# The order of the first loads and of the first matmuls in an S5 and SwiGLU kernel

## The chip, the cores and the metric

The kernel runs on one core of a Trainium2 chip. The metric is the device time of one execution in microseconds. Before the change it is 177.39 us, the median of 3 runs (177.05 to 178.04).

Engine names: TensorE (PE in the profile; PEld is its weight load), VectorE (DVE), ScalarE (ACT), GpSimd (POOL) and SyncE (SP), whose queue issues most transfers.

## What is computed

The input x has 2048 tokens of 512 features, in bf16. Two branches work on its layer norm, and both are added to x:

```python
def _A_ref(x, Lambda_re, Lambda_im, B_re, B_im, C_re, C_im, log_dt, Dskip):
    Lam = Lambda_re + 1j * Lambda_im
    dt = jnp.exp(log_dt)
    Lam_bar = jnp.exp(dt * Lam)
    B_bar = ((Lam_bar - 1.0) / Lam)[:, None] * (B_re + 1j * B_im)
    Bu = jnp.einsum("bld,pd->blp", x + 0j, B_bar)
    hs, h = [], jnp.zeros_like(Bu[:, 0, :])
    for t in range(L):
        h = Lam_bar[None, :] * h + Bu[:, t, :]
        hs.append(h)
    hseq = jnp.stack(hs, 1)
    return 2.0 * jnp.einsum("blp,dp->bld", hseq, C_re + 1j * C_im).real + x * Dskip

def _B_ref(x, w_gate, w_up, w_down):
    return (silu(x @ w_gate) * (x @ w_up)) @ w_down

xn = _layernorm(x)
return x + _A_ref(xn, ...) + _B_ref(xn, ...)
```

The state has 512 entries; gate and up have 1376 features, which is ten blocks of 128 and a last one of 96.

## The kernel before

The tokens are 16 tiles of 128 (`NT`), four to a chunk (`NCH` is 4, `TPC` is 4). The features of x are four blocks of 128 (`KD`; `HK` is half of it, 2). Chunk by chunk the kernel computes the projection with B (`bproj_tile`, eight of four matmuls per chunk), the rotations and scans on VectorE (`ssm_ops`), gate and up (`gateup_tile`, `gateup_last` for the last 96 features), and at the end the product with w_down and C (`out_ffn`, `out_ssm`). Every engine runs its instructions in the order in which the program issues them. VectorE's work of the scans and tables lies in a list with costs (`queue`), and each block of matmuls takes as much from it as it pays for (`pump`); products of gate and up wait in the list `products` until `multiply` issues them.

Chunk 0 is treated differently, and the change touches it alone. While its weights are still on their way, TensorE would have nothing to do; so gate and up of its tiles are computed with the tokens as the stationary operand and 512 features of a weight row as the moving one (`sw_mm`). A weight row here is one block of 128 input features with the first 1024 output features, 256 KB (`load_row`); up has rows 0 to 3 in `wu01`, gate in `wg01`. The rest, output features 1024 to 1375 of both, is `w_end`.

Tiles 0 and 1 do not wait for their layer norm. TensorE transposes the raw tile by a matmul with the identity (`raw_mm`, L237) and subtracts the mean by a second matmul into the same bank (`cT_mean`, L245), whose stationary operand is a row sum that VectorE made (`sum_dve`, L229). ScalarE and VectorE copy the four blocks of the result to `xcT` (`raw_copy`, L252); the scale 1/std is applied when the results leave their banks (`sw_up`, L526; `sw_gate`, L514). `cT_mean(i, k, k + 2)` does two blocks with one matmul. The eight banks of `pair` hold up and gate of two tiles and two groups of 512 features; the transposes borrow banks of it before they are used.

The order of loads on SyncE's queue: tile 0 (L128), the four up rows, gate rows 0 and 1, tile 2, gate row 2, tile 3, gate row 3, `w_end`, chunk 1 of x. Tile 1 is issued on ScalarE's queue (L130), behind a memset of two elements on VectorE. The parameters of the state are three small loads on GpSimd's queue (L145).

The order of TensorE: nine dummy matmuls (L703), transposes of tile 0, its first two means, transposes of tile 1, the other means, then the four up rows, each for tile 0 and tile 1 and both feature groups (`row_mm(0, k)`, four matmuls, L506), then the gate rows. Between them lie the transposes of tile 2, which is centred on VectorE (`center`, L226). After the layer norms of tiles 0 to 3 (`ln_stats` L189, `ln_rstd` L198 and L199, `norm_dve` L207) two transposing transfers on SyncE make `xnT0`, tile 3 first (L258), and behind them the same queue loads and transposes B (`load_bt`, L150). Tiles 2 and 3 and `w_end` follow on TensorE (L506, L805), then chunk 0's projection (L387), then `gateup_last(0)` (L555), which reads `xnT0` and `w_end` in 16 matmuls of 192 columns, then chunk 1's projection. The part of the program from the projection on:

```python
    need("ln0")
    for part in range(2):
        for q in range(NQ):
            bproj_tile(0, part, q)
...
    need("ln1")
    g0_dma(0, fgroups[1][1])
    gateup_last(0)
    pump(GU / 2)
    bproj_chunk(1)
```

Of the kernel before, what the change touches and what calls it, by code (L numbers as in the profile page):

```python
# [23 lines left out]
def kernel(  # L24
# [17 lines left out]
    nc = tc.nc  # L42
# [9 lines left out]
    KD = D // 128  # L52
# [25 lines left out]
    def bank(shape=(128, CW), dtype=F32):  # L78
        return psum.tile(list(shape), dtype, name="ps")

    def flat(ap3):
        return ap3.rearrange("p q j -> p (q j)")

    x_v = A_x[0].rearrange("(n p) d -> p n d", p=128)
    out_v = out[0].rearrange("(n p) d -> p n d", p=128)
    wg_v = B_w_gate.rearrange("(k p) f -> p k f", p=128)
    wu_v = B_w_up.rearrange("(k p) f -> p k f", p=128)


    xall = const.tile([128, NT, D], BF16, name="xall")  # L90
# [5 lines left out]
    wu01 = const.tile([128, KD, FE], BF16, name="wu01")  # L96
# [24 lines left out]
    def load_row(q, t, view, k):  # L121
        q.dma_start(out=t[:, k, :], in_=view[:, k, 0:FE])  # L122

    HK = KD // 2
# [1 line left out]
    make_identity(nc, ident[:])  # L126
    minus_mean = const.tile([128, 128], BF16, name="minus_mean")
    nc.sync.dma_start(out=xall[:, 0, :], in_=x_v[:, 0, :])  # L128
    nc.vector.memset(xall[:, 1, 0:2], 0.0)
    nc.scalar.dma_start(out=xall[:, 1, :], in_=x_v[:, 1, :])  # L130
    nc.scalar.preload_act_table_set("silu_and_others")
    for k in range(KD):
        load_row(nc.sync, wu01, wu_v, k)
    for k in range(HK):
        load_row(nc.sync, wg01, wg_v, k)
# [49 lines left out]
    def by_k(ap):  # L185
        return ap.rearrange("p (k d) -> p k d", d=128)
# [36 lines left out]
    sums = const.tile([128, 2], BF16, name="sums")  # L223
# [4 lines left out]
    def sum_dve(i, dst):  # L228
        nc.vector.scalar_tensor_tensor(out=xnT[:, NCH - 1, i, 0:HW], in0=xall[:, i, 0:HW], scalar=1.0,  # L229
                                       in1=xall[:, i, HW:D], op0=ALU.mult, op1=ALU.add, accum_out=dst)  # L230
# [3 lines left out]
    raw = [pair[0][1] + pair[1][0], pair[1][1] * 2]  # L234

    def cT_mm(ps, src, k, first, stop):
        nc.tensor.matmul(ps[:, k * 128:(k + 1) * 128], lhsT=src[:, k * 128:(k + 1) * 128], rhs=ident[:], start=first,  # L237
                         stop=stop)

    def raw_mm(i):  # L240
        for k in range(KD):
            cT_mm(raw[i][k], xall[:, i, :], k, all(p is not raw[i][k] for p in raw[i][:k]), False)

    def cT_mean(i, *ks):
        nc.tensor.matmul(by_k(raw[i][ks[0]][:])[:, ks[0]:ks[-1] + 1:HK], lhsT=sums[:, i:i + 1].to_broadcast([128, 128]),  # L245
                         rhs=minus_mean[:, None, :].to_broadcast([128, len(ks), 128]), start=False, stop=True)

    def raw_copy(i, k):
        cT_copy(V.tensor_copy if k % 2 else nc.scalar.copy, raw[i][k], i, k, k + 1)

    def cT_copy(copy, ps, i, k0=0, k1=KD):
        copy(out=xcT[:, k0:k1, i * 128:(i + 1) * 128], in_=by_k(ps[:, k0 * 128:k1 * 128]))  # L252
# [21 lines left out]
    V = nc.vector  # L274
# [107 lines left out]
    def bproj_tile(c, part, q):  # L382
        if c not in u_tiles:
            u_tiles[c] = ssm.tile([128, 2, NQ, CW], BF16, name="u16", bufs=2)
        ps = bank()
        for k in range(KD):
            nc.tensor.matmul(ps[:] if c else by_k(ps[:]), lhsT=BT[:, part, k, q * 128:(q + 1) * 128],  # L387
                             rhs=xnT[:, c, k, :] if c else xnT0[:, k], start=(k == 0), stop=(k == KD - 1))
        nc.scalar.copy(out=u_tiles[c][:, part, q, :], in_=ps[:])  # L389
# [67 lines left out]
    products = []  # L457
# [10 lines left out]
    def gu_tile(c):  # L468
        if c not in gu_tiles:
            gu_tiles[c] = gut.tile([128, FT, CW], BF16, name="guT")  # L470
        return gu_tiles[c]
# [8 lines left out]
    def gu_rest(c):  # L480
        return gu_more_rest[:] if c == 2 else gu_tile(c)[:, FT - 1, 0:RT * 128]
# [21 lines left out]
    def sw_mm(ps, groups, gi, i, k0=0, k1=KD):  # L503
        a, b = fgroups[gi]
        for k in range(k0, k1):
            nc.tensor.matmul(ps[:, 0:(b - a) * 128], lhsT=tokens(i, k), rhs=groups[gi][:, k, 0:(b - a) * 128],  # L506
                             start=(k == 0), stop=(k == KD - 1))
# [35 lines left out]
    def g0_dma(a, b):  # L543
        nc.sync.dma_start_transpose(out=runs(gu_tiles[0][:, a:b, :]), in_=g0[:, a:b].rearrange("p f i d -> p (f i d)"))
# [3 lines left out]
    def gateup_last(c):  # L548
        gl = g_last[c % 2][:] if c else g0[:, FT - 1, 0:RT]
        u = up_p.tile([128, RT, 128], BF16, name="ul", bufs=2)  # L550
        for h in range(0, TPC, 2):
            ps = bank()[:, 0:4 * FR].rearrange("p (i w f) -> p i w f", i=2, w=2)
            for i in range(2):
                for k in range(KD):
                    nc.tensor.matmul(ps[:, i],  # L555
                                     lhsT=xnT[:, c, k, (h + i) * 128:(h + i + 1) * 128] if c else xnT0[:, k, h + i, :],
                                     rhs=w_end[:, k, :, FL - FE:FL - FE + FR], start=(k == 0), stop=(k == KD - 1))
            two = slice(h * RB, (h + 2) * RB)
            src = ps.rearrange("p i w (j f) -> p w j i f", f=RB)
            nc.scalar.activation(out=gl[:, :, two].rearrange("p j (i f) -> p j i f", f=RB), in_=src[:, 0], func=ACT.Silu)  # L560
            nc.scalar.copy(out=u[:, :, two].rearrange("p j (i f) -> p j i f", f=RB), in_=src[:, 1])

        def product():
            V.tensor_tensor(out=gl, in0=gl, in1=u[:], op=ALU.mult)
            if c:
                nc.sync.dma_start_transpose(out=gu_rest(c).rearrange("p (n t) -> p n t", t=128),
                                            in_=gl.rearrange("p i d -> p (i d)"))
            else:
                a = fgroups[1][1]
                n = (FT - 1 - a) * TPC + RT  # L570
                nc.sync.dma_start_transpose(
                    out=flat(gu_tile(0)[:, a:FT, :])[:, 0:n * 128].rearrange("p (n t) -> p n t", t=128),
                    in_=g0[:, a:FT].rearrange("p f i d -> p (f i d)")[:, 0:n * 128])
        products.append(product)
# [93 lines left out]
    def step():  # L668
        for item in backlog[0:AHEAD + 1]:
            if item[2] is not None:  # L670
                item[2]()
                item[2] = None
        cost, op, _, _ = backlog.pop(0)
        op()
        owed[0] -= cost

    def pump(us):

        owed[0] += us
        while backlog and owed[0] >= backlog[0][0] * 0.5:  # L680
            step()
        if not backlog:
            owed[0] = 0.0

    def multiply(keep):

        while len(products) > keep:
            products.pop(0)()
            owed[0] -= 0.65

    def need(tag):

        while any(item[3] == tag for item in backlog):
            step()


    GU = 8 * 0.2163
# [29 lines left out]
    dummy(warm, 4, CW)  # L727
    dummy(warm, 5, 128)
    nc.vector.tensor_scalar(out=minus_mean[:], in0=ident[:], scalar1=-1.0 / D, scalar2=None, op0=ALU.mult)
    for i in range(2):  # L730
        sum_dve(i, sums[:, i:i + 1])
    raw_mm(0)
    for k in range(HK):
        cT_mean(0, k)
        raw_copy(0, k)
    raw_mm(1)
    for k in range(HK, KD):
        cT_mean(0, k)
    for k in range(HK):
        cT_mean(1, k, k + HK)  # L740
        raw_copy(1, k)
    for k in range(HK, KD):
        raw_copy(0, k)
    for k in range(HK, KD):
        raw_copy(1, k)

    def row_mm(which, k):
        for i in range(2):
            for gi in range(2):
                sw_mm(pair[which][i][gi], (U, G)[which], gi, i, k, k + 1)  # L750

    for k in range(KD):
        row_mm(0, k)
    for i in range(2):
        ln_stats(i)
        ln_rstd(i, i + 1)
# [3 lines left out]
    for n in range(2):  # L760
        norm_dve(n)
    row_mm(1, 0)
    pp = prm_transpose()
    ln_stats(2)
# [6 lines left out]
    for k in range(1, SW):  # L771
        row_mm(1, k)
# [48 lines left out]
    def bproj_chunk(c):  # L821
        need(f"ln{c}")
        for part in range(2):
            for q in range(NQ):
                bproj_tile(c, part, q)
                pump(BP)
                multiply(0 if q else 1)
# [34 lines left out]
        queue(f"ssm{c}", fwd + back)  # L862

    need("ln0")
    for part in range(2):
        for q in range(NQ):
            bproj_tile(0, part, q)
            pump(BP)
            multiply(0 if q else 1)
# [5 lines left out]
    queue("cf", c_ops())  # L875
    need("ln1")
    g0_dma(0, fgroups[1][1])
    gateup_last(0)
    pump(GU / 2)
    bproj_chunk(1)  # L880
    load_down()
    for part, src in enumerate((A_C_re, A_C_im)):
# [62 lines left out]
```

## Time and profile before

| | us |
|---|---|
| median of 3 runs | 177.39 |
| lowest and highest | 177.05, 178.04 |
| the profiled execution, its own time | 178.12 |
| its span, first to last instruction | 176.0 |
| TensorE busy | 171.0 |
| VectorE busy | 157.4 |
| ScalarE busy | 102.3 |
| all matmuls of chunk 0's last 96 features | 1.32 |

The profile is of one execution. A row of the timeline gives the start and the length in microseconds, the engine, the line of the kernel, the operation, what is written and read, how many instructions were merged into the row, and in brackets how long the engine stood idle before it and what ended that. A row of the chain gives start, length and what the end of the program hung on in that time. A row of transfers ends with the median time from issue to landing. A row of a table of stages gives the stage, its length, the busy time of PE, PEld, DVE, ACT and POOL with the number of instructions, the granted share of TensorE's clock, the busy share of the transfer engines and the GB/s that they moved. [...]

### The profile page before, as it was taken

What the parts mean: (1) busy time and instruction counts of PE and PEld (TensorE: products, weight loads), DVE (VectorE), ACT (ScalarE), POOL (GpSimd) and SP (SyncE); (2) the same over time, 40 slices, a digit from 0 to 9 for tenths busy, and PEclk for the clock granted to TensorE, in tenths of its full rate; (3) what the DMA queues carried; (4) which work ended last, traced back from release to release, by engine and by line L of the source; (5) the groups of instructions that cost most, each with busy time, mean ns of one, the idle gap of its engine ahead of it and who ended that gap; (6) DMA issues with size and microseconds to landing.
All of it is one profiled execution on the core that took longest, in us unless ns stands there. A gap on an engine that the chain in (4) does not pass through costs nothing.

```text
span 176.0 us, 2435 instructions
## 1 busy us (share of the span) xinstructions
PE 171.0 (97%) x878; PEld 82.0 (47%) x894; DVE 157.4 (89%) x260; ACT 102.3 (58%) x188; POOL 27.1 (15%) x36
## 2 busy tenths in 40 slices
PE   8899999999999999999999999999999999999993
PEld 5444445564444464444444444446444444444542
DVE  3767999999999999999999999999999999589642
ACT  3179589794996689976044362014666652983100
POOL 5234110022000000000302500014100000530700
PEclk9999999999999999999999999999999999999999
DMA  5998969999999300220005830006310000597741
GB/s 152 370 342 80 194 110 181 303 202 293 169 207 274 115 4 0 50 61 0 2 4 111 94 34 0 0 4 68 53 22 0 0 4 0 70 164 124 93 89 60
DMA packets 34027, 18.05 MB, mean 103 GB/s; under 512 B 24512, under 2 KB 32832, under 8 KB 33888
## 3 DMA queue, kind: packets, MB, share of 16 engines
q1 hardware_dynamic: 30272, 14.39, 35.0%
q0 software_dynamic: 3456, 3.28, 14.6%
q10 hardware_dynamic: 288, 0.23, 0.4%
q8 instruction: 7, 0.11, 0.3%
q14 instruction: 4, 0.03, 0.1%
HBM read 8.33 MB, written 5.24 MB: 77 GB/s over the span
## 4 chain that ended last, share of the span: by engine, by line
PE 94%; DMA 3%; issue 1%; SPq 0%; ACT 0%; DVE 0%; ACTq 0%
PE ps L462 29%; PE ps L630 20%; PE ps L643 16%; PE ps L387 16%; PE ps L506 7%; PE ps L555 3%; DMA wu<-in_B_w_up_dram 3%; PE ps L805 2%; PE ps L620 2%; ACT u L489 0%; SPq L122 0%; SPq L128 0%; DVE xall L646 0%; PE ps L237 0%; PE ps L278 0%
## 5 line engine op out<-in xcount | busy, mean ns | idle before, releaser
L429 DVE TENSOR_TENSOR_SCAN g<-r_t,car,u 128x512 bf16<-128x512 f32 x24 | 28.8, 1263 | 0.0
L643 PE MATMUL ps<-CF,wt 128*128 128x512 bf16 (+2 forms) x133 | 28.2, 366 | 0.2
L387 PE MATMUL ps<-xnT,BT 128*128 128x512 bf16 x125 | 28.1, 379 | 0.2
L630 PE MATMUL ps<-wd_sb,guT 128*128 128x512 bf16 (+2 forms) x129 | 26.5, 362 | 0.1
L462 PE MATMUL ps<-xnT,wu 128*128 128x512 bf16 x94 | 24.5, 379 | 0.2
L462 PE MATMUL ps<-xnT,wg 128*128 128x512 bf16 x93 | 24.3, 379 | 0.1
L389 ACT CAST u<-ps 128x512 bf16<-128x512 f32 x32 | 17.8, 591 | 5.0 <-PE ps L387 4.1
L489 ACT CAST u<-ps 128x512 bf16<-128x512 f32 x30 | 17.8, 592 | 4.8 <-PE ps L462 4.8
L643 PEld LDWEIGHTS <-wt 128*128 128x128 bf16 x136 | 12.9, 98 | 15.0 <-DVE xall L600 0.4
L387 PEld LDWEIGHTS <-BT 128*128 128x128 bf16 x128 | 12.5, 98 | 14.9 <-DMA BT<-in_A_B_re_dram 0.3
L630 PEld LDWEIGHTS <-guT 128*128 128x128 bf16 x130 | 12.4, 98 | 13.8
L199 POOL TENSOR_TENSOR rstd<-ve,neg_half 128x1 f32<-128x1 f32 (+1 forms) x7 | 7.0, 1001 | 73.0 <-DVE ve L198 72.6
L652 ACT CAST res<-ps 128x512 bf16<-128x512 f32 x12 | 6.9, 582 | 18.5 <-PE ps L643 18.5
L592 ACT ACTIVATE xr<-xall,nb,rstd 128x512 bf16<-128x512 bf16 x16 | 11.8, 804 | 8.7 <-DVE xall L600 5.0
L653 POOL DMA_DIRECT2D out_dram<-res x12 | 10.5, 1043 | 35.6 <-ACT res L652 30.0
L462 PEld LDWEIGHTS <-wu 128*128 128x128 bf16 x96 | 9.4, 98 | 11.3
L488 ACT ACTIVATE guT<-ps 128x512 bf16<-128x512 f32 x20 | 12.1, 604 | 4.0 <-PE ps L462 3.6
L462 PEld LDWEIGHTS <-wg 128*128 128x128 bf16 x96 | 9.3, 98 | 10.6
L212 ACT ACTIVATE xn<-xall,nb,rstd 128x512 bf16<-128x512 bf16 x8 | 6.3, 816 | 8.8 <-DVE nb L202 8.8
L189 DVE BATCH_NORM_STATS2 stats<-xall 128x6 f32<-128x512 bf16 x16 | 10.8, 675 | 0.6 <-DMA xall<-in_A_x_dram 0.6
L462 PE MATMUL ps<-xnT,w_end 128*128 128x512 bf16 x47 | 10.8, 379 | 0.1
L397 DVE TENSOR_TENSOR pm<-g,c 128x2048 bf16<-128x2048 bf16 x8 | 9.8, 1222 | 0.1
(132 smaller groups left out, 235.3 us busy)
## 6 DMA issues: line engine op xcount, KB each, us to landing
out_dram<-in_A_x_dram SPq DMA_DIRECT2D x8, 192.0 KB, 3.2
out_dram<-res POOLq DMA_DIRECT2D x12, 128.0 KB, 3.1
out_dram<-xall POOLq DMA_DIRECT2D x3, 512.0 KB, 6.4
wd_sb<-in_B_w_down_dram SPq DMA_DIRECT2D x1, 1280.0 KB, 7.8
wu<-in_B_w_up_dram SPq DMA_DIRECT2D x4, 256.0 KB, 4.9
wg<-in_B_w_gate_dram SPq DMA_DIRECT2D x4, 256.0 KB, 5.5
xall<-in_A_x_dram SPq DMA_DIRECT2D x1, 1024.0 KB, 7.0
xall<-in_A_x_dram SPq DMA_DIRECT2D x1, 512.0 KB, 6.1
```

The source lines that it names most:

```text
L189: nc.vector.bn_stats(out=stats[:, n, 0, :], in_=xall[:, n, :])
L387: nc.tensor.matmul(ps[:] if c else by_k(ps[:]), lhsT=BT[:, part, k, q * 128:(q + 1) * 128], rhs=xnT[:, c, k, :] if c else xnT0[:, k], star ...
L389: nc.scalar.copy(out=u_tiles[c][:, part, q, :], in_=ps[:])
L429: V.tensor_tensor_scan(out=g()[:, part, q, :], data0=r_t[:, q:q + 1].to_broadcast([128, CW]), data1=u_tiles[c][:, part, q, :], initial=ini ...
L462: nc.tensor.matmul(ps[:fs, lo:hi], lhsT=wslice(groups, fi, k), rhs=xnT[:, c, k, lo:hi], start=(k == 0), stop=(k == KD - 1))
L488: nc.scalar.activation(out=gu(c, fi, fi + 1)[:fs, 0, :], in_=psg[:fs], func=ACT.Silu)
L489: nc.scalar.copy(out=u_pair[c][:fs, fi % 2, :], in_=psu[:fs])
L506: nc.tensor.matmul(ps[:, 0:(b - a) * 128], lhsT=tokens(i, k), rhs=groups[gi][:, k, 0:(b - a) * 128], start=(k == 0), stop=(k == KD - 1))
L592: nc.scalar.activation(out=box["xr"][:], in_=xall[:, n, :], func=ACT.Identity, scale=rstd[:, n:n + 1], bias=nb[:, n:n + 1])
L630: nc.tensor.matmul(o_tiles[n, b][:, 0:hi - lo], lhsT=gu(c, fi, fi + 1)[:, 0, i * 128:(i + 1) * 128], rhs=wd_sb[:, fi, lo:hi], start=(fi == ...
L643: nc.tensor.matmul(o[:, 0:hi - lo], lhsT=w_tiles[c][:, part, q, i * 128:(i + 1) * 128], rhs=CF[:, part, q, lo:hi], start=False, stop=(part ...
L653: nc.gpsimd.dma_start(out=out_v[:, n, lo:hi], in_=res[:, lo:hi], accum_op=ALU.add)
```

## The change

Four things are changed.

1. Tile 1's load moves from ScalarE's queue to SyncE's, behind up rows 0 and 1 and in front of up rows 2 and 3. The memset before it goes.
2. TensorE transposes tile 0 and subtracts all four means, then does up rows 0 and 1 for tile 0 alone. Then come tile 1's transposes and means, row 2 for tile 0, rows 0 to 2 for tile 1, and row 3 for both.
3. VectorE forms tile 1's row sum behind its two copies of tile 0. Its copies of tile 1 go to ScalarE, which now does six of eight.
4. `gateup_last(0)` moves in front of chunk 0's projection. Its product and the transfer behind it keep their place in the order of VectorE and SyncE: the entry is taken out of `products` and put back later.

```diff
     nc.sync.dma_start(out=xall[:, 0, :], in_=x_v[:, 0, :])
-    nc.vector.memset(xall[:, 1, 0:2], 0.0)
-    nc.scalar.dma_start(out=xall[:, 1, :], in_=x_v[:, 1, :])
     nc.scalar.preload_act_table_set("silu_and_others")
-    for k in range(KD):
+    for k in range(HK):
+        load_row(nc.sync, wu01, wu_v, k)
+    nc.sync.dma_start(out=xall[:, 1, :], in_=x_v[:, 1, :])
+    for k in range(HK, KD):
         load_row(nc.sync, wu01, wu_v, k)
...
     def raw_copy(i, k):
-        cT_copy(V.tensor_copy if k % 2 else nc.scalar.copy, raw[i][k], i, k, k + 1)
+        cT_copy(V.tensor_copy if k % 2 and i == 0 else nc.scalar.copy, raw[i][k], i, k, k + 1)
...
-    for i in range(2):
-        sum_dve(i, sums[:, i:i + 1])
+    def row_mm(which, k, tiles=range(2)):
+        for i in tiles:
+            for gi in range(2):
+                sw_mm(pair[which][i][gi], (U, G)[which], gi, i, k, k + 1)
+
+    sum_dve(0, sums[:, 0:1])
     raw_mm(0)
-    for k in range(HK):
+    for k in range(KD):
         cT_mean(0, k)
         raw_copy(0, k)
+    for k in range(HK):
+        row_mm(0, k, (0,))
+    sum_dve(1, sums[:, 1:2])
     raw_mm(1)
-    for k in range(HK, KD):
-        cT_mean(0, k)
     for k in range(HK):
         cT_mean(1, k, k + HK)
+    for k in range(KD):
         raw_copy(1, k)
-    for k in range(HK, KD):
-        raw_copy(0, k)
-    for k in range(HK, KD):
-        raw_copy(1, k)
-
-    def row_mm(which, k):
-        for i in range(2):
-            for gi in range(2):
-                sw_mm(pair[which][i][gi], (U, G)[which], gi, i, k, k + 1)
-
-    for k in range(KD):
-        row_mm(0, k)
+    row_mm(0, HK, (0,))
+    for k in range(HK + 1):
+        row_mm(0, k, (1,))
+    row_mm(0, KD - 1)
...
     need("ln0")
+    gateup_last(0)
+    pump(GU / 2)
+    last0 = products.pop()
     for part in range(2):
...
     g0_dma(0, fgroups[1][1])
-    gateup_last(0)
-    pump(GU / 2)
+    products.append(last0)
     bproj_chunk(1)
```

## The prediction

> **What bounds the kernel now.** I began with the page's busy times, went on to the chain that ended last in order of time, then to the waits of TensorE, and last to a table of stages cut where the chain changes its kind.
>
> ```profile
> span 176.0 us, 2435 instructions
> PE 171.0 (97%) x878; PEld 82.0 (47%) x894; DVE 157.4 (89%) x260; ACT 102.3 (58%) x188; POOL 27.1 (15%) x36
> 1.65 4.80 DMA wu<-in_B_w_up_dram
> 6.49 3.61 PE ps L506 x16
> 23.33 6.91 PE ps L387 x32
> 30.24 1.32 PE ps L555 x16
> PE ps L506 <- DMA wu<-in_B_w_up_dram: 0.6, 1, 0.6
> 4.82:6.49 1.67, 1.07 (x5) 0.43 (x4) 1.39 (x5) 0.60 (x3) 0.00 (x0) 1.00 0.97 352
> 9.08:23.33 14.25, 14.14 (x69) 6.55 (x70) 11.65 (x35) 11.34 (x25) 4.99 (x6) 1.00 0.98 196
> 30.24:173.60 143.36, 142.29 (x741) 68.07 (x752) 134.28 (x192) 82.08 (x148) 18.27 (x18) 1.00 0.43 82
> ```
>
> TensorE is busy for 97% of the span. In the stage rows the second number is the stage's length and the third TensorE's busy time. TensorE is busy 14.14 of 14.25 us and 142.29 of 143.36 us, so everything behind 9.08 us is one queue of matmuls. Its only wait on data is 0.6 us for row 1 of the up weights, in the stage that ends at 6.49. The chain says the same: a transfer from 1.65 to 6.45, then matmuls. Whatever the change does to the moment at which TensorE has finished the four up rows of tiles 0 and 1 (9.08 us, the start of the first gate row), it does to the end, as long as nothing later becomes a new wait.
>
> The transfers and the work around that wait:
>
> ```profile
> 0.74 0.40 SPq L128 DMA_DIRECT2D xall<-in_A_x_dram  x1
> 0.90 0.37 ACTq L130 DMA_DIRECT2D xall<-in_A_x_dram  x1
> 1.20 1.83 SPq L122 DMA_DIRECT2D wu<-in_B_w_up_dram  x4
> xall<-in_A_x_dram SPq DMA_DIRECT2D x1, 128.0 KB, 2.3
> xall<-in_A_x_dram ACTq DMA_DIRECT2D x1, 128.0 KB, 2.5
> wu<-in_B_w_up_dram SPq DMA_DIRECT2D x1, 256.0 KB, 2.9
> wu<-in_B_w_up_dram SPq DMA_DIRECT2D x1, 256.0 KB, 4.8
> wu<-in_B_w_up_dram SPq DMA_DIRECT2D x1, 256.0 KB, 5.0
> wu<-in_B_w_up_dram SPq DMA_DIRECT2D x1, 256.0 KB, 5.2
> 3.00:4.00 1.00, 1.00 (x11) 0.78 (x10) 0.85 (x5) 0.11 (x1) 0.54 (x2) 1.00 0.96 250
> 4.00:5.00 1.00, 1.00 (x9) 0.84 (x8) 0.29 (x1) 0.30 (x2) 0.00 (x0) 1.00 0.99 273
> 7.00:8.00 1.00, 1.00 (x6) 0.41 (x5) 0.93 (x4) 0.00 (x0) 0.58 (x2) 1.00 1.06 395
> ```
>
> The last column of a transfer is the time from issue to landing. So tile 0 lands at 0.74 + 2.3 = 3.04, tile 1 at 3.40, and the up rows (issued at 1.20, 1.65 and, by the same steps of some 0.47, at 2.13 and 2.60) at 4.1, 6.45, 7.13 and 7.8. Row 1 comes 2.35 us behind row 0, rows 2 and 3 only 0.68 behind the one before. The transfer engines are busy throughout (0.96 and 0.99 of 1) but move 250 and 273 GB/s, against 395 later: 256 KB at 395 GB/s is 0.66 us, so row 1 lost about 1.7 us in packets that took long. The profile does not show why.
>
> **The change part by part.** The profiled execution's own time is 178.12 (span 176.0 and 2.1 around it), 0.73 above the median of 177.39 and 0.08 above the highest of the three runs. I make the sum as a difference and add it to the median.
>
> ```profile
> 3.07 0.42 DVE L229 SCALAR_TENSOR_TENSOR xnT<-xall 128x256 bf16<-128x256 bf16 x1 [1.53 <-DMA xall<-in_A_x_dram]
> 3.56 0.39 PE L245 MATMUL ps<-minus_mean,sums 128*128 128x128 bf16 x2
> 4.18 0.85 PE L245 MATMUL ps<-minus_mean,sums 128*128 128x128 bf16 x4
> 3.89 0.27 ACT L252 CAST CF<-ps 128x128 bf16<-128x128 f32 x1 [1.30 <-PE ps L245]
> 6.49 2.75 PE L506 MATMUL ps<-wu,CF 128*128 128x512 bf16 x12 [0.60 <-DMA wu<-in_B_w_up_dram]
> 9.08 1.03 PE L506 MATMUL ps<-wg,CF 128*128 128x512 bf16 x4
> 11.72 0.39 PE L237 MATMUL ps<-ident,CF 128*128 128x128 bf16 x4
> L506 PE MATMUL ps<-wu,CF 128*128 128x512 bf16 x24 | 5.9, 381 | 0.6 <-DMA wu<-in_B_w_up_dram 0.6
> ```
>
> *The move of tile 1 in SyncE's queue.* Tile 1's 128 KB go from ScalarE's queue, ahead of row 0, to SyncE's, behind row 1. Rows 0 and 1 lose 128 KB ahead of them: 0.33 us at 395 GB/s, so row 1 lands at 6.12 if its long packets stay. Tile 1 then has the same bytes ahead of it that row 1 had before (tile 0, rows 0 and 1, itself), so it lands where row 1 landed, at 6.45. One issue of 0.47 more on SyncE moves every later issue by that, and rows 2 and 3 keep their bytes, so I leave them at 7.13 and 7.8. ScalarE loses an issue of 0.37 with nothing waiting behind it, and VectorE a 2-element memset: nothing.
>
> *TensorE's order.* First the spacing of its matmuls. Twelve of 512 columns and the step to the next row take 9.08 - 6.49 = 2.59, so 0.216 each, and one lasts 381 ns, so that it trails its successor's start by 0.165. Without that tail the four transposes of 11.72 are 0.06 apart ((0.39 - 0.165) / 4), and the pieces of 4.18, two of 128 and two of 256 columns, take 0.11 for each 128 columns ((0.85 - 0.165) / 6). Early in the program TensorE runs at half its later speed: 0.43 for 512 columns.
>
> Until row 1 lands, before had 16 pieces of small work and four row-0 matmuls; now it has tile 0's transposes and means and two row-0 matmuls. Those end at about 4.9: means from 3.56, the copy 0.33 behind the first mean and 0.27 long, so row 0 begins near 4.1 and its two matmuls take 0.43 each. TensorE then stands from 4.9 to 6.12. Two row-1 matmuls and tile 1's four transposes end by 6.8. The means of tile 1 need its sum, which VectorE may start only when tile 1 lands: from start of the sum to the first mean is 3.56 - 3.07 = 0.49, so 6.45 + 0.03 + 0.49 = 6.97. The two means of 256 columns cost 4 x 0.06 = 0.24 at full and 4 x 0.11 = 0.44 at half speed; I take full speed, which the matmuls behind 6.49 had, and 0.22 for them since the 0.06 is rounded up. Then stand 2 + 6 + 4 = 12 matmuls, as many as before behind row 1's landing, 2.59. The sum is 6.97 + 0.22 + 2.59 = 9.78, against 9.08: **+0.70**. Row 2 (7.13) and row 3 (7.8) are there before their matmuls (7.19 and 8.9). All four copies of tile 1 now go to ScalarE: first at 6.97 + 0.33 + 0.27 = 7.57, while two row-2 matmuls run to 7.62, and then one each 0.27 at most against two matmuls of 0.43: at nothing, and 0.1 if the first copy is that late.
>
> *What is queued behind VectorE's new wait.* Behind tile 1's sum stand both tiles' statistics, their normalisations, and through them the third and fourth tile, the transposes on SyncE, and the loads of B.
>
> ```profile
> 5.67 0.68 DVE L189 BATCH_NORM_STATS2 stats<-xall 128x6 f32<-128x512 bf16 x1
> 8.54 0.41 DVE L207 TENSOR_SCALAR CF<-xall,mv,rstd 128x512 bf16<-128x512 bf16 x1 [0.46 <-POOL rstd L199]
> 9.55 0.69 DVE L189 BATCH_NORM_STATS2 stats<-xall 128x6 f32<-128x512 bf16 x1 [0.60 <-DMA xall<-in_A_x_dram]
> 15.77 4.41 SPq L150 DMA_TRANSPOSE BT<-in_A_B_re_dram  x1
> BT<-in_A_B_re_dram SPq DMA_TRANSPOSE x1, 7.3
> xnT<-CF SPq DMA_TRANSPOSE x1, 5.8
> 13.02 2.70 SPq L258 DMA_TRANSPOSE xnT<-CF  x2
> ```
>
> The statistics start at 7.0 for 5.67 and the second normalisation ends 8.95 - 5.67 = 3.28 later, at 10.28; the third tile's statistics, which waited for their transfer until 9.55, now start 0.73 late. So the transposes and the first B land 0.73 late: B at 15.77 + 7.3 + 0.73 = 23.8. Its user, the first projection, moves to 23.33 + 0.70 + 1.32 = 25.35, behind the 16 small matmuls. Slack 1.55, where it was 23.33 - 23.07 = 0.26.
>
> *The 96 features in front.* 16 matmuls and four evacuations move as they are (1.32 us from 30.24 to 23.33 in the chain); they need the transposed tiles 0 to 2, landed by 14.4 + 5.8 + 0.73 = 20.9 (the second of the two issues that take 2.70 from 13.02 starts half-way), and TensorE is there at 24.0. Their product and its transfer stay where they were in VectorE's and SyncE's order, so the loads behind them on SyncE's queue are not moved past anything. Chunk 0's scan work waits for the projection 1.32 later; VectorE reached it at 38.15, long behind 30.24 + 1.32:
>
> ```profile
> 38.15 1.22 DVE L397 TENSOR_TENSOR pm<-u,s 128x2048 bf16<-128x2048 bf16 x1
> 23.10 6.65 PEld L387 LDWEIGHTS <-BT 128*128 128x128 bf16 x32 [0.26 <-DMA BT<-in_A_B_re_dram]
> ```
>
> Cost nothing, hidden by the 6.6 us of tables and statistics that VectorE does in between; without that cover 1.32. Its use is the 0.26 wait of the weight load, which cost TensorE nothing here; in a run with a later B it would save what B is late, up to 1.32.
>
> **The rivals.** *A, the sum:* +0.70, 177.39 + 0.70 = 178.1, between 177.8 (row 1 less late) and 178.6 (a copy late, means at half speed).
>
> *B, no long packets, before and after.* The median is 0.73 under the profiled run, and that is about the stall. Then row 1 is there near 4.75, tile 1 near 4.6, and both orders keep TensorE going: what is left is the wait for tile 0's copy (from the last mean at 3.9 to 4.1, worth 0.1 at half speed) and the copy of tile 1, against 0.1 for an earlier tile 0. 177.3 to 177.7, so 177.5.
>
> *C, tile 1's separate queue made row 1's packets long.* For it: they begin right behind that transfer. Against: tile 1 had landed by 3.40 and the slow time goes on to 5. Then the changed kernel loses the stall (0.6 by the wait, 0.8 as 1.67 less four matmuls of 0.216; I take 0.8) and perhaps a late B: 177.39 - 0.8 = 176.6, and 176.3 with the 0.26 of B's wait. [...]
>
> *D, A and a cold TensorE; slower.* Its place is the new idle time of 1.2 us before row 1, twice the old one.
>
> ```profile
> L703 PE MATMUL ps<-const-bfloat16-1.0 128*128 128x512 bf16 x4 | 1.9, 619 | 0.8 <-PEq L929 0.8
> ```
>
> Early matmuls of 512 columns last 619 ns, later ones 381. If TensorE is slow again or still behind that idle time, each of the next matmuls costs 0.21 more: four to eight of them give 0.9 to 1.7 on top of A, 179.0 to 179.8, and with five 179.2. It decides against the 0.5% from one on. [...]
>
> **How the numbers follow.** A 0.42, because the slow time lies where row 1 lies in both orders; B 0.20, C 0.20, D 0.18. The time is A's, 178.1. 0.5% (0.89 us) is about what a measurement of this kernel can tell from no change: faster is under 176.5, slower over 178.28. Of A 0.42 lies above (0.18), of D nearly all (0.17), so slower 0.36 with a little of B; half of C and a tenth of B make faster 0.12; same 0.52. The range from 176.6 to 179.2 leaves out half of C and half of D. A's own is 177.8 to 178.6.
>
> **What would show it.** After: tile 1's landing near 6.45, the sum of VectorE directly behind it, a wait of TensorE of about 1.2 us for row 1, the first gate row at 9.78, and the first projection without a wait for B. Right for the wrong reason it would be if TensorE lost the time at B or at a bank. The forecast is wrong if row 1 lands under 5 us (B or C), if the matmuls behind it are 0.43 apart (D), or if the first gate row starts at 9.1 or sooner.

## The result and the profile after

| | before, us | after, us |
|---|---|---|
| median of 19 runs each | 177.53 | 178.08 |
| lowest and highest | 177.05, 178.43 | 177.56, 180.19 |
| the profiled execution, its own time | 178.12 | 178.05 |
| its span | 176.0 | 176.0 |
| TensorE busy | 171.0 | 171.0 |

The ratio of after to before is 1.0035, with an interval from 1.0020 to 1.0049. So the change costs 0.6 us (0.35% of 177.5), between 0.36 and 0.87: a small loss, within the 0.5% that was called no change. The two profiled executions have the same span although the medians of the two kernels differ: the profile of before is an execution 0.6 above its median, that of after one at its median. So the two traces alone must not be read as "nothing changed".

The busy times of the page and the waits of TensorE, after:

```profile
PE 171.0 (97%) x878; PEld 81.8 (46%) x894; DVE 156.9 (89%) x257; ACT 103.2 (59%) x190; POOL 27.2 (15%) x36
PE ps L507 <- DMA wu<-in_B_w_up_dram: 0.6, 1, 0.6
```

The chain that ended last, after, for the first 32 us (start, length, what it hung on):

```profile
1.65 3.59 DMA wu<-in_B_w_up_dram
5.28 0.59 PE ps L507 x2
5.87 0.22 PE ps L238 x4
6.12 0.39 PE ps L246 x2
6.54 3.61 PE ps L507 x16
...
23.38 1.32 PE ps L556 x16
24.70 7.12 PE ps L388 x33
```

The transfer at the head of the chain still is the row issued at 1.65, which is row 1, but it lands at 5.24 where it landed at 6.45. Behind it stand two matmuls of row 1, tile 1's four transposes and two means, and the twelve matmuls that the prediction counted. The 96 features (L556) lie ahead of the projection (L388), at their old 1.32.

TensorE's timeline at that place, after:

```profile
4.63 1.23 PE L507 MATMUL ps<-wu,CF 128*128 128x512 bf16 x4 [0.60 <-DMA wu<-in_B_w_up_dram]
5.71 0.39 PE L238 MATMUL ps<-ident,xall 128*128 128x128 bf16 x4
6.12 0.39 PE L246 MATMUL ps<-minus_mean,sums 128*128 128x256 bf16 x2
6.54 2.75 PE L507 MATMUL ps<-wu,CF 128*128 128x512 bf16 x12
9.13 1.03 PE L507 MATMUL ps<-wg,CF 128*128 128x512 bf16 x4
```

And VectorE's:

```profile
5.63 0.43 DVE L230 SCALAR_TENSOR_TENSOR xnT<-xall 128x256 bf16<-128x256 bf16 x1 [1.27 <-DMA xall<-in_A_x_dram]
...
5.98 0.69 DVE L190 BATCH_NORM_STATS2 stats<-xall 128x6 f32<-128x512 bf16 x1
```

The wait of 0.6 is not for row 1. The four matmuls that start at 4.63 contain both rows of tile 0, so the wait before them is for row 0, which landed at 4.59 here. The two matmuls of row 1 follow at 5.28 by the chain, right behind its landing and 0.2 later than the two of row 0 (0.216 each) would have let them. Tile 1 landed at 5.61, and VectorE's sum follows 0.02 later, the first mean 0.49 behind the sum, as predicted from the row of tile 0. From the first mean to the row-2 matmuls are 0.42, not 0.22. Row 2 landed at 6.50, 0.04 ahead of them, the same distance as between the landing and the first matmul of row 0 here (4.59 and 4.63) and of row 1 in before (6.45 and 6.49); so by these distances it was row 2 that the twelve matmuls waited for last, although the list of waits does not have it. The first gate row starts at 9.13.

The stages behind that point are those of before:

```profile
9.13:23.38 14.25, 14.14 (x70) 6.64 (x71) 12.12 (x38) 11.77 (x25) 4.99 (x6) 1.00 1.07 224
31.60:173.60 142.00, 140.98 (x725) 66.82 (x736) 132.60 (x190) 81.28 (x143) 18.29 (x18) 1.00 0.43 78
```

TensorE is busy 14.14 of the 14.25 us behind the first gate row, as before, and misses 1.02 us of the last 142. From the start of the first gate row to the end of the last matmul 164.19 us go by in both (9.08 to 173.27 and 9.13 to 173.32). So this one number, the start of the first gate row, tells what each trace will take. The table has it for eight traces, in us; the landings are the arrival of the last packet in the trace, "time less start" is the run's own time minus the start of the first gate row.

| trace | row 0 | row 1 | tile 1 | row 2 | first gate row | run's time | time less start |
|---|---|---|---|---|---|---|---|
| before | 4.10 | 6.45 | 3.38 | 7.11 | 9.08 | 178.12 | 169.04 |
| before, second trace | 3.97 | 5.87 | 3.32 | 6.52 | 8.50 | 177.52 | 169.02 |
| only the 96 features moved | 3.98 | 6.26 | 3.21 | 6.92 | 8.89 | 177.93 | 169.04 |
| after | 4.59 | 5.24 | 5.61 | 6.50 | 9.13 | 178.05 | 168.92 |
| after, second trace | 3.85 | 4.60 | 5.16 | 6.12 | 9.27 | 178.25 | 168.98 |
| after without the 96 features | 4.02 | 4.72 | 5.98 | 6.63 | 9.31 | 178.38 | 169.07 |
| only the order of TensorE | 4.31 | 5.96 | 3.19 | 6.75 | 9.46 | 178.54 | 169.08 |
| only the load of tile 1 | 3.89 | 4.59 | 5.75 | 6.50 | 11.64 | 180.49 | 168.85 |

The last column is the same within 0.23 us while the times differ by 3. In these eight traces nearly all of the difference arises before the first gate row.

### The profile page after: what moved, and what is told of

Its sections match the earlier page's. It is cut to its first block, busy times and chain, and to the rows that moved or that the text cites. A ratio compares the mean times of both kernels' runs of the same rounds, so it can differ in the third digit from the quotient of the medians.

```text
span 176.0 us, 2433 instructions
## 1 busy us (share of the span) xinstructions
PE 171.0 (97%) x878; PEld 81.8 (46%) x894; DVE 156.9 (89%) x257; ACT 103.2 (59%) x190; POOL 27.2 (15%) x36
## 3 DMA queue, kind: packets, MB, share of 16 engines
HBM read 8.33 MB, written 5.24 MB: 77 GB/s over the span
## 4 chain that ended last, share of the span: by engine, by line
PE 95%; DMA 2%; issue 1%; SPq 0%; ACT 0%; DVE 0%; ACTq 0%
PE ps L463 29%; PE ps L631 20%; PE ps L644 16%; PE ps L388 16%; PE ps L507 8%; PE ps L556 3%; DMA wu<-in_B_w_up_dram 2%; PE ps L804 2%; PE ps L621 2%; ACT u L490 0%; PE ps L238 0%; SPq L122 0%; SPq L128 0%; PE ps L246 0%; DVE xall L647 0%
## 5 line engine op out<-in xcount | busy, mean ns | idle before, releaser
L388 PE MATMUL ps<-xnT,BT 128*128 128x512 bf16 x125 | 28.0, 379 | 0.2
L388 PEld LDWEIGHTS <-BT 128*128 128x128 bf16 x128 | 12.5, 98 | 14.9
```

## The experiments

Each ratio is to the kernel before, run in turn on the same chip. The theories that the expectations speak of are the prediction's A to D and one that came with the first traces, S: the three small loads of GpSimd's queue, which run beside the rows, make the packets long.

**The parts one by one: the front alone.** The changed kernel with the 96 features put back behind the projection.

```diff
     need("ln0")
-    gateup_last(0)
-    pump(GU / 2)
-    last0 = products.pop()
...
     g0_dma(0, fgroups[1][1])
-    products.append(last0)
+    gateup_last(0)
+    pump(GU / 2)
     bproj_chunk(1)
```

> The changed kernel without the move of chunk 0's last 96 features: load and order of tile 1 as changed, the rest as before. Theory 1 (the 0.55 us lie in the front, where tile 1's work now stands behind late transfers): ratio to before 1.002 to 1.005, first gate row at 9.1 or later. Theory 2 (the 0.55 us come from the 96 features in front of the projection): ratio 0.999 to 1.001.

Median of 12 runs 178.36 (177.60 to 178.99), ratio 1.0030 [1.0011, 1.0050]: the whole loss. Its chain, the front:

```profile
2.13 3.85 DMA xall<-in_A_x_dram
...
6.02 0.51 PE ps L238 x4
6.53 0.35 PE ps L246 x2
```

Here the chain hangs on tile 1 (landed at 5.98) and not on a weight row. The first gate row starts at 9.31, which is 5.98 + 3.33: the prediction's own 0.03 + 0.49 + 0.22 + 2.59 with another landing. Row 2, which landed at 6.63, would have given nearly the same: 6.63 + 0.04 + 2.59 = 9.26.

**The 96 features alone.** The kernel before with `gateup_last(0)` in front of the projection, as in the change.

```diff
     need("ln0")
+    gateup_last(0)
+    pump(GU / 2)
+    last0 = products.pop()
...
     g0_dma(0, fgroups[1][1])
-    gateup_last(0)
-    pump(GU / 2)
+    products.append(last0)
     bproj_chunk(1)
```

> The kernel before with only the 16 matmuls of chunk 0's last 96 features in front of its first projection. Theory 1 (front): ratio 0.998 to 1.0005; under 1 if B is late in some runs. Theory 2 (the 96 features): ratio 1.002 to 1.005, with an idle stretch of TensorE between 22 and 35 us that the kernel before has not.

Median of 12 runs 177.58 (177.17 to 178.24), ratio 0.9992 [0.9975, 1.0008]. No loss, and no gain that can be told from none. In the changed kernel's trace, B could not have stopped the projection with or without it. Its issue and its landing, after:

```profile
15.57 3.01 SPq L151 DMA_TRANSPOSE BT<-in_A_B_re_dram  x1
BT<-in_A_B_re_dram SPq DMA_TRANSPOSE x1, 5.5
```

15.57 + 5.5 = 21.1, and TensorE is ready for it at 23.38 without the 96 features.

**The load alone.** The kernel before, tile 1 loaded behind rows 0 and 1, TensorE's order unchanged.

```diff
-    nc.vector.memset(xall[:, 1, 0:2], 0.0)
-    nc.scalar.dma_start(out=xall[:, 1, :], in_=x_v[:, 1, :])
     nc.scalar.preload_act_table_set("silu_and_others")
-    for k in range(KD):
+    for k in range(HK):
+        load_row(nc.sync, wu01, wu_v, k)
+    nc.sync.dma_start(out=xall[:, 1, :], in_=x_v[:, 1, :])
+    for k in range(HK, KD):
         load_row(nc.sync, wu01, wu_v, k)
```

> The kernel before with only tile 1's load moved behind up rows 0 and 1 on SyncE's queue; TensorE's order as before, so tile 1's transposes stand in front of all up rows. Theory 1a (the loss is tile 1's late landing): TensorE waits for tile 1 until about 4.6 to 6.5 and then does its four transposes, means and 16 matmuls: first gate row at 8.8 to 10.6, ratio 1.003 to 1.009. Theory 1b (the loss is the order alone, the load matters little): ratio under 1.002.

Six runs: 178.67, 178.99, 179.40 and 180.49, 180.84, 180.96; ratio 1.0121 [1.0079, 1.0163]. The traced run is of the second group. Its waits and three stages of 3.41 us (length, TensorE's busy time, ..., and third from the end the granted clock):

```profile
PE ps L238 <- DMA xall<-in_A_x_dram: 2.0, 1, 2.0
```

```profile
3.80:7.21 3.41, 1.45 (x13) 0.83 (x13) 1.15 (x6) 0.84 (x4) 0.00 (x0) 1.00 0.97 313
7.22:10.63 3.41, 3.41 (x10) 1.19 (x9) 2.81 (x10) 0.00 (x0) 1.24 (x2) 0.50 1.05 378
10.63:14.04 3.41, 3.41 (x18) 1.53 (x17) 2.59 (x9) 2.42 (x4) 1.64 (x3) 1.00 0.85 272
```

```profile
11.64 1.03 PE L507 MATMUL ps<-wg,CF 128*128 128x512 bf16 x4
```

TensorE, which has nothing else to do until tile 1 comes in this order, waits 2.0 us for it. In the 3.41 us that hold this wait (from 3.80, where the clock became full) it is busy 1.45. In the next 3.41 us (7.22 to 10.63), with TensorE busy throughout, the granted clock is 0.50, and then 1.00 again. The sixteen matmuls of the up rows start at 6.50 and the first gate row at 11.64; that is 5.14 us, where sixteen at 0.216 take 3.46: 1.7 us lost. That is why the first gate row (11.64) and the ratio lie above what was expected. This is what rival D said: a TensorE that is slow again behind an idle time. Eight matmuls of 0.43 fill the 3.41 us at 0.50, and 1.7 is the price that it gave for eight. The 3.41 us ahead of the half clock were not empty: TensorE was busy for 43% of them.

**The order alone.** The kernel before, TensorE's and VectorE's order and the copies as in the change, tile 1 still on ScalarE's queue.

```diff
+    sum_dve(0, sums[:, 0:1])
     raw_mm(0)
-    for k in range(HK):
+    for k in range(KD):
         cT_mean(0, k)
         raw_copy(0, k)
+    for k in range(HK):
+        row_mm(0, k, (0,))
+    sum_dve(1, sums[:, 1:2])
     raw_mm(1)
...
+    row_mm(0, HK, (0,))
+    for k in range(HK + 1):
+        row_mm(0, k, (1,))
+    row_mm(0, KD - 1)
```

> The kernel before with only TensorE's and VectorE's new order; tile 1 on ScalarE's queue as before, so that it lands near 3.4. Theory 1a (late landing of tile 1): tile 1 never waits for its load, ratio 0.999 to 1.001 in executions with an early row 1. Theory 1b (order): tile 1's transposes, means and two matmuls stand behind row 1, which costs up to 0.9 where row 1 lands at 6.5 and 0.1 where it lands before 5: ratio 1.001 to 1.005.

Median of 12 runs 178.40 (177.53 to 180.41, three runs between 180.1 and 180.4), ratio 1.0041 [1.0010, 1.0072]. TensorE's timeline:

```profile
6.00 0.59 PE L506 MATMUL ps<-wu,CF 128*128 128x512 bf16 x2 [0.69 <-DMA wu<-in_B_w_up_dram]
6.43 0.39 PE L237 MATMUL ps<-ident,xall 128*128 128x128 bf16 x4
6.65 0.38 PE L245 MATMUL ps<-minus_mean,sums 128*128 128x256 bf16 x2
6.87 2.75 PE L506 MATMUL ps<-wu,CF 128*128 128x512 bf16 x12
9.46 0.81 PE L506 MATMUL ps<-wg,CF 128*128 128x512 bf16 x3
```

Row 1 landed at 5.96. In before's order the first gate row starts 0.04 + 2.59 behind it (6.45 and 9.08), which would be 8.59. Here it starts at 9.46: the two matmuls of row 1 and tile 1's transposes and means, 0.87 from 6.00 to 6.87, which before had been done while row 1 was on its way, now stand behind it. So the order costs 0.87 when row 1 is the late one. Not all of it is tile 1's work: row 2 landed at 6.75, so the twelve matmuls could not have begun before 6.79 in any case.

**Before and after once more.** One more trace of each, unchanged.

> The kernel before once more, for a second trace. If the slow packets belong to the time from 3.4 to 5 us and not to one execution: row 1 of the up weights lands between 5.7 and 6.5, more than 1.5 behind row 0, and the first gate row starts 2.63 behind that. If the first trace was an odd one (rival B): row 1 lands before 5 and the first gate row starts at 8.2 to 8.5.

> The changed kernel once more. By the sum's chain (tile 1's landing, 0.52 to its first mean, 0.22 for the means, 2.59 for 12 matmuls) the first gate row starts 3.33 to 3.55 behind tile 1's landing, which lies between 5.6 and 6.0. If row 0 or the copies of tile 1 set it instead, it does not follow tile 1.

177.52 and 178.25, in the table above. Before did as expected; after did not: tile 1 landed at 5.16, sooner than expected, and the first gate row started 4.11 behind it. TensorE's timeline of before, second trace:

```profile
4.79 3.87 PE L506 MATMUL ps<-wu,CF 128*128 128x512 bf16 x16
8.50 1.03 PE L506 MATMUL ps<-wg,CF 128*128 128x512 bf16 x4
```

And its chain:

```profile
1.66 4.21 DMA wu<-in_B_w_up_dram
5.91 3.61 PE ps L506 x16
```

Row 1 came at 5.87, about when the four matmuls of row 0 were done: TensorE's waits show none for it, and yet row 1's landing is where the chain begins (5.91 + 2.59 = 8.50). TensorE's timeline of after, second trace:

```profile
4.07 1.89 PE L507 MATMUL ps<-wu,CF 128*128 128x512 bf16 x4
5.75 0.63 PE L238 MATMUL ps<-ident,xall 128*128 128x128 bf16 x4
6.18 0.63 PE L246 MATMUL ps<-minus_mean,sums 128*128 128x256 bf16 x2
6.61 2.83 PE L507 MATMUL ps<-wu,CF 128*128 128x512 bf16 x12
```

Here row 0 came at 3.85 and TensorE waited for no load, but its clock was granted in full only from 6.74 (4.87 in the second trace of before). Until then it ran at half speed: four matmuls of 512 columns take 5.75 - 4.07 = 1.68, which is 0.42 each. The first gate row started at 9.27.

**GpSimd's loads.** The three parameter loads go from GpSimd's queue to SyncE's, behind the four up rows, in the kernel before and in the changed one.

```diff
+    prm_rows = const.tile([128, 128], BF16, name="prm_rows")
+    nc.gpsimd.memset(prm_rows[:], 0.0)
+    for i, v in enumerate((A_Lambda_re, A_Lambda_im, A_log_dt)):
+        nc.sync.dma_start(out=prm_rows[i * NQ:(i + 1) * NQ, :], in_=v.rearrange("(q j) -> q j", j=128))
     for k in range(HK):
         load_row(nc.sync, wg01, wg_v, k)
```

> The kernel before with the three 1 KB loads of the state's parameters on SyncE's queue, behind the four up rows, instead of GpSimd's. Theory S (the three loads of GpSimd's queue, issued from 1.78 to 3.5, make the packets of the rows slow between 3.4 and 5): row 1 lands near 4.75, TensorE has no wait for it, first gate row at 8.2 to 8.5, ratio 0.994 to 0.998. Theory H (the rows are slow by themselves, from memory): row 1 lands at 5.7 to 6.5 as before, ratio 0.999 to 1.001.

> The changed kernel with the same three loads on SyncE's queue behind the four up rows. Theory S: tile 1 lands near 4.6, first gate row at 8.3 to 8.6, ratio to the kernel before 0.996 to 1.000. Theory H: tile 1 at 5.6 to 6.0, ratio 1.002 to 1.005 as the changed kernel.

Ratios 1.0041 [1.0023, 1.0059] and 1.0082 [1.0065, 1.0098], medians 178.43 and 179.08. With nothing but SyncE's queue and tile 1 running, row 1 still landed at 5.74 in the first, 1.77 behind row 0, and tile 1 at 6.12 in the second, 1.52 behind row 1. S falls: the slow time is there without these loads. Theory H about fits the landings but not the ratios, for both kernels are slower than it said. The parameters do not come too late: TensorE reads them at 9.91 in the first (9.94 in before) and at 10.32 in the second (9.99 in after), each time right behind the first gate row and without a wait.

```profile
9.91 0.22 PE L278 MATMUL ps<-ident,prm_rows 128*128 128x128 bf16 x1
```

From the first gate row (9.05 and 9.46) to the end of the last matmul 164.19 us go by, as in before and after. What is lost on top of the front lies behind that: the span ends 3.06 and 3.29 behind the last matmul, 2.71 and 2.72 in before and after. The runs do not show why, so they say no more of the change.

**The idle time filled.** The load alone, with five matmuls of constants in the place where TensorE waits, into a bank that is written over later.

```diff
         raw_copy(0, k)
+    dummy(pair[1][1][0], 5, CW)
     raw_mm(1)
```

> The kernel with only tile 1's load moved, and five matmuls of 512 columns on constants (their result is overwritten by tile 1's transposes) in the 2 us in which TensorE waits for tile 1. Clock theory (rival D: a window of 3.4 us in which TensorE did too little sets its clock to half for the next 3.4 us, worth 1.7 us): no run over 179.5, median 178.6 to 179.1, a chip-granted clock that stays at 1 behind its first rise, first gate row at 9.4 to 10.2. If the slow runs of that kernel have another cause (late tile 1): half of the runs stay over 180.

Median of 6 runs 179.03 (178.77 to 179.20), ratio 1.0086 [1.0071, 1.0101]. No run is near 180.5 any more, where three of six were; if the filling changed nothing, the three slow runs of the twelve would all fall on the side without it once in eleven times. TensorE's timeline:

```profile
3.61 1.57 PE L704 MATMUL ps<-const-bfloat16-1.0 128*128 128x512 bf16 x5
6.41 3.62 PE L507 MATMUL ps<-wu,CF 128*128 128x512 bf16 x16
9.86 0.38 PE L507 MATMUL ps<-wg,CF 128*128 128x512 bf16 x1
```

Sixteen matmuls in 9.86 - 6.41 = 3.45, which is 0.216 each, at a clock that stays full. The first gate row is still 0.8 later than in before's trace: tile 1 landed at 5.66, and all sixteen matmuls stand behind it.

**Another order with before's loads.** Tile 1's transposes and means between row 0 and row 1 of tile 0, so that they are done while row 1 is on its way.

```diff
+    row_mm(0, 0, (0,))
+    sum_dve(1, sums[:, 1:2])
     raw_mm(1)
...
+    row_mm(0, 1, (0,))
+    row_mm(0, HK, (0,))
+    for k in range(HK + 1):
+        row_mm(0, k, (1,))
+    row_mm(0, KD - 1)
```

> The new order with tile 1 on ScalarE's queue, but tile 1's sum, transposes and means in front of row 1's two matmuls for tile 0 instead of behind them; 14 matmuls are left behind row 1's landing where the kernel before leaves 12 and the new order 14 with the transposes and means. Sum theory (what is moved behind row 1 costs its own length): first gate row 3.06 behind row 1's landing (2.63 before, 3.50 with the new order), ratio 1.001 to 1.003, between the kernel before and the new order. If the order's loss is something else (a copy, a bank, the clock): first gate row over 3.3 behind row 1.

Median of 8 runs 178.43 (177.62 to 178.85), ratio 1.0049 [1.0032, 1.0067], more than expected. TensorE's timeline:

```profile
6.27 0.59 PE L506 MATMUL ps<-wu,CF 128*128 128x512 bf16 x2 [0.94 <-DMA wu<-in_B_w_up_dram]
7.27 2.75 PE L506 MATMUL ps<-wu,CF 128*128 128x512 bf16 x12 [0.41 <-DMA wu<-in_B_w_up_dram]
```

Behind row 1 come only two matmuls, 0.43, before row 2 is asked for, and row 2 lands 1.0 behind row 1. So row 2 takes row 1's place as the late one, with twelve matmuls still behind it, the number that before has behind row 1. The first gate row starts at 7.23 + 0.04 + 2.59 = 9.86, which is 3.63 behind row 1 and not the 3.06 of the sum theory: that sum had left row 2 out. An order is bad that leaves little work between one late row and the next.

**Copies of tile 1 shared again.** The changed kernel with VectorE taking two of tile 1's four copies, as before.

```diff
-        cT_copy(V.tensor_copy if k % 2 and i == 0 else nc.scalar.copy, raw[i][k], i, k, k + 1)
+        cT_copy(V.tensor_copy if k % 2 else nc.scalar.copy, raw[i][k], i, k, k + 1)
```

> The changed kernel, with every second copy of tile 1 on VectorE as before the change. Sum theory: the copies are hidden behind the matmuls of row 2, so the time is that of the changed kernel, ratio to before 1.002 to 1.005; VectorE's statistics start some 0.3 to 0.6 later, at no cost, since B has 0.3 to 1.5 of slack. If the four copies on ScalarE hold TensorE up: ratio under 1.002.

Median of 6 runs 178.97 (178.60 to 179.40), ratio 1.0084 [1.0066, 1.0101]. The first gate row starts at 8.97, sooner than in the changed kernel, and yet the kernel is 0.9 slower. One new entry in TensorE's waits:

```profile
PE ps L388 <- DMA xnT<-xn: 0.4, 1, 0.4
```

The chain at that place:

```profile
86.46 0.17 DVE ve L199
...
94.41 5.45 DMA xnT<-xn
99.91 7.08 PE ps L388 x32
```

And VectorE's timeline at the front:

```profile
6.98 0.69 DVE L190 BATCH_NORM_STATS2 stats<-xall 128x6 f32<-128x512 bf16 x1
```

VectorE's statistics start at 6.98 where the changed kernel has 5.98. The 1.0 us is carried along VectorE's list to the statistics of chunk 3, whose transposed tiles are issued at 94.41 (93.25 in the changed kernel) and land at 99.87 (97.5). TensorE uses them at 99.91 after a wait; the changed kernel starts there at 99.49. Of the 2.0 us between 97.5 and 99.49, 1.16 went to the later issue; the transfer itself took 5.45 against 4.3, and whether that belongs to the later start is open. In this trace 164.79 us lie between the first gate row and the end of the last matmul, 0.6 more than in all the others; the rest of the 0.9 between the medians is not traced. So the front of VectorE has a slack of its own, and it is spent 90 us later.

**Tile 1 second on SyncE's queue.** The kernel before, tile 1 directly behind tile 0 on the same queue.

```diff
-    nc.vector.memset(xall[:, 1, 0:2], 0.0)
-    nc.scalar.dma_start(out=xall[:, 1, :], in_=x_v[:, 1, :])
+    nc.sync.dma_start(out=xall[:, 1, :], in_=x_v[:, 1, :])
```

> The kernel before, in its order, with tile 1's load on SyncE's queue directly behind tile 0's, in front of the up rows, and no load on ScalarE's queue. In the traces so far the first 768 KB (tiles 0 and 1, rows 0 and 1) had landed between 5.74 and 6.45 where tile 1 was on ScalarE's queue and between 5.16 and 6.12 where all of it was on SyncE's. If one queue alone is faster: row 1 lands at 5.2 to 6.1, first gate row 2.63 behind it, at 7.8 to 8.7, ratio 0.996 to 0.999, faster than both kernels. If not, or if the one issue of 0.47 more in front of row 0 makes it later: row 1 at 5.9 to 6.7, ratio 1.000 to 1.003.

Median of 12 runs 177.80 (177.24 to 179.09), ratio 1.0011 [0.9990, 1.0032]: no gain. TensorE's timeline:

```profile
5.43 3.84 PE L505 MATMUL ps<-wu,CF 128*128 128x512 bf16 x16 [0.54 <-DMA wu<-in_B_w_up_dram]
9.11 1.03 PE L505 MATMUL ps<-wg,CF 128*128 128x512 bf16 x4
```

And the stages in which the packets are long, with the share of the transfer engines and the GB/s at the end:

```profile
3.00:4.00 1.00, 1.00 (x12) 0.94 (x11) 0.92 (x5) 0.25 (x1) 0.54 (x2) 1.00 0.82 234
4.00:5.00 1.00, 0.89 (x7) 0.55 (x5) 0.22 (x2) 0.30 (x3) 0.00 (x0) 1.00 0.97 278
```

With one queue for all the large loads, it is row 0 that is late in this trace, 5.39, 2.06 behind tile 1 (3.33), and row 1 follows only 0.68 later. So the slow time does not belong to a transfer or to a queue. It lies mostly between 3 and 6 us of the program, and whatever is on its way then is late: row 1 in before, row 0, tile 1 or row 2 in after, row 0 here.

No version here beats the kernel before.

## Why the prediction was right, and where it was not

*What bounds the kernel*: right. The moment of the first gate row decides, and the rest is a constant (169.0 within 0.2). Nothing later became a new wait of the changed kernel.

*The forecast, A*: right in direction and place, +0.70 forecast, +0.55 between the medians and +0.62 [0.36, 0.87] by the ratio. The loss is in the front: the front alone has all of it, the 96 features none. The mechanism is A's in kind: small work that was hidden behind a late row now stands behind a late transfer. But A's own chain, from tile 1's landing to the first gate row, is what set the time in only one of the three traces with the changed front, the front alone. In the profiled run it was row 2, in the second trace the half clock. That the number came so near is in part luck, as the next three paragraphs show.

*Tile 1's landing*: the mis-sized term. The prediction had it land at 6.45, where row 1 had landed. In the seven traces with this load order it landed at 5.16 to 6.12, 5.70 on average. Row 1 in the six traces with the old order landed at 5.74 to 6.45, 6.08 on average. So tile 1 is about 0.4 earlier than row 1 was, and the profile from which the 6.45 was read was the latest of the six. That this profile was a late one dropped out of the difference, for before's first gate row is also earlier in its other traces (8.50 and 8.89 beside 9.08); the 0.4 did not. The forecast's time came from adding a difference to the median, not to the profiled run, and that is why it held.

*The work behind the landing*: 3.33 predicted; 3.33 measured in the front alone, 3.52 in the profiled run, where row 2 came at 6.50, and 4.11 in the second trace, where the clock was not yet full. Before's work behind row 1 is 2.63. So the sum with the measured landings gives a loss of 0.70 - 0.38, some 0.3; row 2 and the clock can make up the rest, in shares that the runs do not show. A late clock is not special to the change: in the kernel before with the parameters on SyncE's queue it was full only from 6.47, and the first gate row started at 9.05, though row 1 had landed at 5.74.

*Row 2 "there before its matmuls"*: the prediction had it 0.06 ahead of them (7.13 and 7.19) and then left it out. It is a second path of the same length: row 2's landing, 0.04, and the twelve matmuls of 2.59. This is the first gate row by either path, beside the measured one:

| trace | tile 1 + 3.33 | row 2 + 2.63 | measured |
|---|---|---|---|
| after | 8.94 | 9.13 | 9.13 |
| after without the 96 features | 9.31 | 9.26 | 9.31 |
| after, copies shared | 8.96 | 8.95 | 8.97 |
| after, parameters on SyncE's queue | 9.45 | 9.40 | 9.46 |
| after, second trace | 8.49 | 8.75 | 9.27 |

The later of the two paths gives the start in the first four. Had tile 1's work behind its landing cost nothing, row 2 would have held these four back all but 0.1 as long. The last twelve matmuls wait for row 1 in before, which is 768 KB into the loads, and for row 2 in the changed order, 1 MB into them. No run separates the two paths.

*Row 1 at 6.12 and TensorE idle for 1.2*: wrong. Row 1 landed at 4.60 to 5.24, and TensorE waited 0.6 for row 0 and 0.2 for row 1 in one trace, and in the other two its waits show neither. The step "row 1 lands at 6.12 if its long packets stay" failed at its condition: they stay in time, not with row 1.

*B*, no long packets in typical runs: the slow time was in every trace, with varying length, so its premise fell. *C*, tile 1's own queue as the cause, fell too: with tile 1 on SyncE's queue, in the changed kernel and right behind tile 0, and with the parameters there as well, the slow time was still there, and no kernel gained.

*D*, the half clock: not the usual case, and real. It was traced in the kernel with the load alone (0.50 for 3.41 us), and with the idle time filled no run of six showed it. One of the changed kernel's 19 runs took 180.19, and three of twelve with the order alone over 180; that these are D is argued from the size (some 2.1 above the median of the other runs, where the two groups of the load alone are 1.7 apart), and none of them was traced.

*The 96 features*: cost nothing and saved nothing, as predicted. *The copies on ScalarE* at nothing: right, and better than that, since the shared version is slower by another 0.5% (178.97 against 178.08).

*What was queued behind VectorE's new wait*: the forecast asked only for B (23.8 against 25.35; it was 21.1 against 24.54, without a wait). It did not look at the use 90 us later, chunk 3's transposes, which the shared copies showed to be the nearer bound: VectorE 1.0 later already cost there. The changed kernel is spared because its statistics start 0.3 later than before's (5.98 and 5.67), not 1.3 as forecast; in the front alone they start at 6.35, and there is no wait either. Had tile 1 landed at 6.45, the time would probably have come out above the forecast for this reason.

## What to carry to other kernels

A landing read from one profile is one draw (row 1 landed at 5.74 to 6.45 in six traces with the old order of loads): take a second trace of the same kernel before a difference of half a microsecond is built on it, and add the difference to the median. To hide a late transfer, ask not which one is late but which work can be done until the slow time is over; work that needs nothing from it should stand ahead of it, and between one late row and the next there must be enough to do. A delay of an engine off the path can come due much later, here 90 us, so follow it to every place where the bounding engine reads its results.

## What the runs showed of the hardware that was not expected

The first transfers of this program were slow. In each of the fourteen traces one of the stages from 3 to 4, 4 to 5 and 5 to 6 us moves only 202 to 298 GB/s (250 from 3 to 4 in before, 274 from 5 to 6 in after), with the engines busy for 0.68 or more of it (0.96 and 1.04 there). From 8 to 9 us it is 378 to 402 (394 and 381), but for the two kernels with the parameters on SyncE's queue. The loss falls on whatever transfer is on its way: up to 2.35 us between the landings of two rows (4.10 and 6.45), when the rows behind them in the same trace are 0.65 to 0.68 apart. It was there with several queues and with one for all the large loads (row 0 landed 2.06 behind tile 1), and with and without GpSimd's small loads (without them row 1 landed 1.77 behind row 0); why the packets take long stays open.

TensorE's clock became full at a moment that differs from run to run, 3.5 to 6.7 us after the start in the thirteen traces that record it (3.80 in the load alone, 4.91 in before, 6.74 in the second trace of after), with the same nine dummy matmuls ahead. In the load alone a stretch of 3.41 us with 1.45 busy was followed by 3.41 us at half the clock (0.50); stretches of the same length, also cut from the moment of the full clock, with 2.06 busy (the other order with before's loads) and 2.35 (the 96 features alone) were not.
